# A main part played from one written list, with relu evictions over one or two PSUM banks and input loads as words of the list

## The chip, the cores and the metric

The kernel runs on one NeuronCore of one Trainium2 chip. The metric is the device time of one execution in microseconds (us). Engines are named as the profile names them: PE is TensorE (matmuls; PEld is its weight load), DVE is VectorE, ACT is ScalarE, POOL is GpSimd, SP is SyncE, which here only issues DMAs.

## The reference

Two stages follow each other. The first is induced attention on `x` (4 batches of 12544 rows of 128), with 32 inducing rows `I`:

```python
def mab(q, kv):
    s = scale * (q @ kv.transpose(0, 2, 1))
    s = s - s.max(-1, keepdims=True)
    a = np.exp(s)
    a /= a.sum(-1, keepdims=True) + 1e-09
    return a @ kv
h = mab(I, x)
return mab(x, h)
```

The second takes the 50176 resulting rows, with three weights, as

```python
h1 = x @ w1
h2 = x @ w2
g = np.maximum(h1, h2)
return g @ w_out
```

where `w1` and `w2` are 128x1024 and `w_out` is 1024x128. The output is 50176x128 in float32.

## The kernel before, in words

**Algebra.** max(h1, h2) = h1 + relu(h2 - h1), so the second stage is x·(w1·w_out) + relu(x·(w2 - w1))·w_out. As a row of the attention's output is (weights over 32 inducing rows) @ h, divided by its denominator, `w2 - w1` and `w1·w_out` are first multiplied by h (32 rows): `hwd` and `m1`. Per chunk of 128 rows PE then makes 8 relu inputs (128 x 128 each) from the exponentials `e2` (32 rows deep) and `hwd`, evicts them from PSUM with relu to f16, multiplies the 8 relu tiles with the 8 pieces of `w_out` on the full array and accumulates them in one PSUM region, adds the linear part `e2·m1`, divides by the denominator in the last eviction and stores.

**Tiling.** A batch has 98 chunks. Chunks are staged in 28 blocks of up to 16 chunks: one block's scores are made by four column tiles of PE (`stage`, 128x32 tiles) and exponentiated by ACT into one `e2` tile in which row quarter q (partitions 32q to 32q+31) holds up to four chunks. The relu inputs of the four quarters are made side by side by four row tiles (32x128) of PE. One *unit* is one PSUM bank (512 f32 columns) of relu inputs of one quarter; 784 units in all. A *group* is the chunks of one quarter of one block: up to four chunks in one output bank, 8 products per chunk; 108 groups, 3136 products. PSUM has 8 banks, `psall[:, 0..7, :]`, which units, groups, stages and all the rest share. PE changes its tile shape between products (128x128), units (32x128) and stages or scores (128x32).

**Phase 1 of the next batch** runs within the main part of the current one: seven loads of x (POOL's queue, float32 in DRAM to f16), DMA transposes of x into `xT` (SP's queue, words `x`), scores against the inducing rows (`c`), DMA transposes of their exponentials (`t`), sums (`a`), the rest (`r`), then small steps (`e`, `h`, `w`, `m`) that give `hwd` and `m1`. Batch 0 has its phase 1 in a head of its own, before 22 us.

**What sets the order.** Every engine runs its instructions in the order in which the kernel records them (`tc.manual_schedule`), and waits for others by semaphores. Before, the order of the main part comes from `ORDER`, a string of words, together with a planner: `Clock` estimates when each engine and bank is free; `phase(n, vector)` picks up to n quarters that have a unit to make, the bank that is free first for each, and an order of matmuls by estimated tile times, with a bit of `vector` per unit for its evicting engine (DVE or ACT); a number N means N products (`final_one`); `keep_busy` puts filler matmuls on `warm` in front of products that the clock expects to wait; `bank()` takes the bank that the clock holds to be free first. Weight steps (`weights_3`, and the third step of `small_hwd(0, ...)`) put fillers too. `relu_out` can evict two neighbouring banks as one instruction where a unit is held for the next (`hold`), but no word of `ORDER` asks for it: before, all relu evictions are of one bank.

**Denominators.** For most blocks a DMA transpose of `e2` (SP) feeds five additions and one power with exponent -1 on POOL (`turn_e2`, words `g`); for the others PE multiplies `e2` with a matrix of ones and DVE takes the reciprocal (`dens`). Group evictions (`evict_group`) wait for them; `EVICT` says for each group whether DVE evicts it in one instruction (0) or ACT in one per chunk (1). Six output buffers `osbs` are stored from SP's queue.

**Loads before.** All seven loads of batch b+1 for b = 1 and 2 are issued in a row at the end of the last sum (`pool_accum`, `last`), behind a copy into `pace` on POOL that waits for that sum. The loads of batch 1 are issued in the head.

Lines that the steps below touch: 840 and 619 (warm-up and filler matmuls), 662 (product of the weights), 712 (stage), 945 (filler of `keep_busy`), 989 (products), 1205 (units and linear part), 1110 and 1107 (relu eviction on ACT and DVE), 1024 and 1031 (group eviction on DVE and ACT), 776 and 780 (POOL's denominators), 228 (loads), 241 (transposes of x).

Of the kernel before, what the change touches and what calls it, by code (L numbers as in the profile page):

```python
# [9 lines left out]
F16 = mybir.dt.float16  # L10
# [6 lines left out]
INF = 1e9  # L17
# [90 lines left out]
class Quarter:  # L108


    def __init__(self, b, c0, w):
        self.b, self.c0, self.w = b, c0, w
        self.subs = {1: [1], 2: [2], 3: [2, 1], 4: [4]}[w]


class Block:


    def __init__(self, quarters, full=()):
        self.quarters = quarters  # L120
        self.width = max(qu.w for qu in quarters if qu)
        self.b = [qu.b for qu in quarters if qu][0]
        self.staged = None
        self.first = None
        self.divided = 0.0
        self.rp = None
        self.units = []
        self.done = {}
        self.relu = {}
        self.last_group = {}  # L130
        self.groups = []
        for q, qu in enumerate(quarters):
            jobs = []
            t0 = 0
            for w in qu.subs if qu else []:
                for u in range(2 * w):
                    jobs.append((q, t0, w, u))
                t0 += w
            self.units.append(jobs)
            if qu:  # L140
                self.groups.append(Group(self, [(q, t) for t in range(qu.w)], q in full))


class Group:
    def __init__(self, blk, chunks, full):
        self.blk, self.chunks, self.full = blk, chunks, full
        self.q = chunks[0][0]
        self.bank = self.ps = None
        self.started = self.linear = False
        self.order, self.parts = [], []  # L150
        for q, t0, w, u in blk.units[self.q]:
            jpb = 4 // w
            self.parts.append((t0, u))
            self.order += [(jpb * u + jj, t0 + t) for jj in range(jpb) for t in range(w)]
# [3 lines left out]
def kernel(  # L158
# [37 lines left out]
    relus = [big.tile([128, 2, 4096], F16, name=f"relus{q}", tag=f"relus{q}") for q in range(4)]  # L196
    relu1 = [big.tile([128, 1024], F16, name=f"relu1_{q}", tag=f"relu1_{q}") for q in range(2)]
    osbs = big.tile([128, NOUT, 4, C], F32, name="osbs", tag="osbs")

# [23 lines left out]
    def load_x(b, i, after=None):  # L223
        k0, n = parts[b][i]
        if after is not None:

            nc.gpsimd.tensor_copy(out=pace, in_=after)
        nc.gpsimd.dma_start(out=xn_at[b, i][:, 0:n, :], in_=xr[b, :, k0 : k0 + n, :])  # L228
        if b:
            issued = ck.on_pool(ck.pe, 0.55)  # L230
            if i == 0 and b > 1:
                ck.loading = issued - 0.55
            st[b]["ld", i] = ck.loading + 6.3 + 2.72 * i if b > 1 else 25.7 + 2.5 * i
# [4 lines left out]
    def transpose_x_dma(b, j):  # L238
# [3 lines left out]
        landed = ck.on_sp(st[b]["ld", i], "x7" if n == 7 else "x14")  # L242
        for k in range(k0, k0 + n):
            st[b]["T", k] = landed

    identity16 = consts.tile([128, 128], F16, name="identity16")
    head16 = relus[3][:, 0, :]
# [10 lines left out]
    wf = relus[0][:, 0, :].bitcast(F32)  # L258
    w1f, w2f = wf[:, 0:J], wf[:, J : 2 * J]
    w1s = relus[1][:, 0, :]  # L260
# [8 lines left out]
    pace = consts.tile([128, 1], F32, name="pace")  # L269

    with tc.manual_schedule(engines={ET.PE, ET.DVE, ET.Activation, ET.Pool, ET.SP}):

        xf = relus[2][:, 0, 0 : 256 * P1].bitcast(F32)
# [119 lines left out]
        def pool_scores(b, u):  # L393
            if u == 0:
                st[b]["es"] = smp.tile([128, NU], F32, name=f"es_{b}", tag="esu")
            bi, ps = bank([128, 512])
            ck.wait(ck.bank[bi], "p1")
# [10 lines left out]
            ck.feed(8)  # L408
            end = ck.run(0.226, "col")
            if u % 2 == 0:  # L410
                st[b]["pair", u // 2] = etp.tile([128, 2, 512], F16, name=f"eu_{b}_{u}", tag="eu", bufs=3)
            eu = st[b]["pair", u // 2][:, u % 2, :]
            nc.scalar.activation(  # L413
                out=eu, in_=ps, func=AF.Exp, scale=scale, accum_out=st[b]["es"][:, u : u + 1]
            )
            ck.bank[bi] = ck.on_act(end, 0.575)
            st[b]["eu", u] = eu, ck.bank[bi]

        def pool_rest(b):

            bi, ps = bank([128, 512])
            ck.wait(ck.bank[bi], "p1")
# [900 lines left out]
```

## Time and profile before

| | |
|---|---|
| median of 3 runs | 314.52 us (314.47 to 314.9) |
| the profiled execution's span, first to last instruction | 312.9 us |
| mean granted PE clock | 0.998 |
| PE busy | 306.0 us (98%), 5316 matmuls |
| ACT busy | 280.7 us (90%) |
| DVE busy | 273.1 us (87%) |
| POOL busy | 122.6 us (39%) |

How rows are read. A group of instructions has "xcount | busy us, mean ns of one | idle time before them and what ended it". A row of waits has the waiting engine and line, what it waited for, and us in total, times, longest. A row of the timeline has start, duration from the first to the last of merged instructions, engine, line and operation; its duration holds the pipeline's depth, so starts are compared with starts. A row of stretches has the stretch, then busy time and count for PE, PEld, DVE, ACT and POOL, then the granted PE clock, the DMA engines' share and GB/s. A busy PE is a PE with a matmul in its pipeline.

### The profile page before, as it was taken

The page shows a single profiled execution, that of the slowest core. Times are in us where ns is not written, and L with a number is a line of the kernel's source. Part 1 is how long each engine was busy: PE and PEld are TensorE (multiplying, and loading weights), DVE is VectorE, ACT ScalarE, POOL GpSimd, SP SyncE. Part 2 cuts the span into 40 slices and gives each one's busy share as a digit, 9 for nine tenths or more (in the row PEclk, how much of TensorE's full clock was granted, in tenths as well). Part 3 has the DMA queues.
Part 4 walks back from the last instruction along what each step waited for, and adds up shares of the span by engine and source line. Part 5 has one row for each costly group of instructions (what it writes and reads, how often), then busy time and mean ns, then how long its engine had stood idle before and what let it go on. Part 6 is the DMA issues. An engine that isn't in the chain of part 4 may idle for free.

```text
span 312.9 us, 12567 instructions
## 1 busy us (share of the span) xinstructions
PE 306.0 (98%) x5316; PEld 239.4 (77%) x5316; DVE 273.1 (87%) x485; ACT 280.7 (90%) x581; POOL 122.6 (39%) x183
## 2 busy tenths in 40 slices
PE   6999999999999999999999999999999999999996
PEld 2875777777877777778877887778778877788885
DVE  2458999999889999988999998999999899989894
ACT  3668999999989989999999999989999899998875
POOL 7374007910530006677500565139205743288000
PEclk9999999999999999999999999999999999999999
DMA  7999999999399999989699999993422522342223
GB/s 206 208 255 203 218 214 192 167 231 232 107 204 244 256 212 202 212 199 218 136 241 256 185 241 200 194 229 114 131 86 103 153 102 87 118 130 103 103 88 136
DMA packets 80793, 55.69 MB, mean 178 GB/s; under 512 B 62272, under 2 KB 65632, under 8 KB 80736
## 3 DMA queue, kind: packets, MB, share of 16 engines
q1 hardware_dynamic: 74768, 41.19, 56.5%
q0 software_dynamic: 5968, 13.70, 22.6%
q8 instruction: 41, 0.67, 0.9%
q14 instruction: 16, 0.13, 0.1%
HBM read 27.28 MB, written 25.69 MB: 169 GB/s over the span
## 4 chain that ended last, share of the span: by engine, by line
PE 94%; DMA 3%; DVE 1%; issue 1%; POOL 0%; ACT 0%; POOLq 0%
PE psall L989 61%; PE psall L1205 23%; DMA xn<-in_x_dram 3%; PE psall L712 2%; PE psall L458 1%; PE psall L399 1%; PE psall L309 1%; PE psall L371 1%; PE psall L325 1%; DVE relus L1107 1%; PE psall L571 1%; PE psall L504 0%; PE psall L362 0%; DVE hwd L575 0%; PE psall L819 0%
## 5 line engine op out<-in xcount | busy, mean ns | idle before, releaser
L1110 ACT ACTIVATE relus<-psall 128x512 f16<-128x512 f32 x468 | 239.2, 620 | 15.4 <-PE psall L1205 14.4
L1107 DVE TENSOR_SCALAR relus<-psall 128x512 f16<-128x512 f32 x308 | 195.5, 683 | 16.6 <-PE psall L1205 15.7
L989 PE MATMUL psall<-woutp,relus 128*128 128x128 f16 x3104 | 203.7, 220 | 0.0
L989 PEld LDWEIGHTS <-relus 128*128 128x128 f16 x3104 | 174.9, 98 | 33.1 <-issue 27.3
L1205 PE MATMUL psall<-e,hwd 32*128 32x512 f16 (+2 forms) x840 | 81.1, 362 | 0.0
L776 POOL TENSOR_TENSOR half<-ed 128x256 f32<-128x256 f16 (+2 forms) x22 | 13.4, 611 | 145.5 <-DMA ed<-e 145.5
L780 POOL TENSOR_TENSOR rd<-den,minus 128x16 f32<-128x16 f32 (+2 forms) x22 | 57.8, 2628 | 1.7
L1024 DVE TENSOR_TENSOR osbs<-psall,rd 128x512 f32<-128x512 f32 (+1 forms) x80 | 50.9, 637 | 4.3 <-PE psall L1205 1.3
L1205 PEld LDWEIGHTS <-hwd 32*128 32x128 f16 x880 | 27.9, 91 | 11.7 <-issue 2.3
L1205 PE MATMUL psall<-m,e 32*128 32x128 f16 x372 | 36.6, 216 | 0.0
L1205 PEld LDWEIGHTS <-e 32*128 32x128 f16 x372 | 22.2, 92 | 9.6 <-issue 2.0
L776 POOL TENSOR_TENSOR half<-half 128x32 f32<-128x32 f32 (+4 forms) x66 | 21.4, 324 | 5.2
L228 POOL DMA_DIRECT2D xn<-in_x_dram x32 | 17.8, 569 | 5.7 <-DMA xn<-in_x_dram 4.3
L1024 DVE TENSOR_TENSOR osbs<-psall,rp 128x512 f32<-128x512 f32 (+3 forms) x24 | 15.6, 649 | 0.5 <-PE psall L1205 0.4
L313 DVE COPY xT<-psall 128x512 f16<-128x512 f16 (+3 forms) x12 | 5.7, 485 | 8.6 <-PE psall L309 8.4
L413 ACT ACTIVATE eu<-psall 128x512 f16<-128x512 f32 x18 | 10.8, 612 | 0.3 <-PE psall L399 0.2
L725 ACT ACTIVATE e<-psall 128x512 f16<-128x512 f32 (+2 forms) x21 | 10.9, 574 | 0.1
L316 ACT COPY xT<-psall 128x768 f16<-128x768 f16 (+3 forms) x10 | 5.8, 576 | 4.6 <-PE psall L309 4.5
L309 PE MATMUL psall<-identity,xn 128*128 128x128 f16 x98 | 7.5, 219 | 1.5 <-DMA xn<-in_x_dram 1.0
L712 PE MATMUL psall<-xT,hT 128*32 128x512 f16 (+3 forms) x110 | 8.4, 362 | 0.0
L309 PEld LDWEIGHTS <-xn 128*128 128x128 f16 x98 | 5.5, 97 | 3.1 <-DMA xn<-in_x_dram 1.4
L399 PE MATMUL psall<-xT,inducingT 128*32 128x512 f16 x72 | 6.4, 381 | 0.0
(114 smaller groups left out, 129.8 us busy)
## 6 DMA issues: line engine op xcount, KB each, us to landing
out_dram<-osbs SPq DMA_DIRECT2D x90, 256.0 KB, 2.9
xn<-in_x_dram POOLq DMA_DIRECT2D x24, 448.0 KB, 9.9
out_dram<-osbs SPq DMA_DIRECT2D x10, 128.0 KB, 4.3
relus<-in_moe_w_dram POOLq DMA_DIRECT2D x4, 256.0 KB, 5.7
xn<-in_x_dram POOLq DMA_DIRECT2D x4, 224.0 KB, 10.3
xT<-xn SPq DMA_TRANSPOSE x33, 4.3
relus<-in_x_dram SPq DMA_DIRECT2D x1, 512.0 KB, 4.0
relus<-in_x_dram SPq DMA_DIRECT2D x1, 384.0 KB, 4.4
```

What stands on the lines that cost most here:

```text
L228: nc.gpsimd.dma_start(out=xn_at[b, i][:, 0:n, :], in_=xr[b, :, k0 : k0 + n, :])
L309: nc.tensor.transpose(ps[:, j, :], xn[:, g + j, :], identity16)
L413: nc.scalar.activation(out=eu, in_=ps, func=AF.Exp, scale=scale, accum_out=st[b]["es"][:, u : u + 1])
L712: nc.tensor.matmul(out=ps[32 * q : 32 * (q + 1), 128 * t : 128 * (t + n)], lhsT=hq, rhs=xT[:, c : c + n, :], start=True, stop=True, tile_p ...
L725: nc.scalar.activation(out=blk.e2[:, 0 : 128 * wd], in_=ps[:, 0 : 128 * wd], func=AF.Exp, scale=st[0]["rs"] if blk.b == 0 else scale,)
L776: nc.gpsimd.tensor_tensor(out=dst, in0=cur[:, :, 0:n], in1=cur[:, :, n : 2 * n], op=ALU.add)
L780: nc.gpsimd.tensor_tensor(out=rp[:, 0:wd, :].rearrange("p t q -> p (t q)"), in0=den[:, 0 : 4 * wd], in1=minus1[:, 0 : 4 * wd], op=ALU.pow,)
L989: nc.tensor.matmul(out=g.ps[lo:hi, 128 * c : 128 * (c + 1)], lhsT=relu[:, lo:hi], rhs=woutp[:, jb, :], start=not g.started, stop=(state["m ...
L1024: nc.vector.tensor_mul(osb[:, 0:m, :], g.ps[:, 0 : m * C].rearrange("p (s c) -> p s c", s=m), g.blk.rp[:, t0 : t0 + m, q : q + 1].broadcas ...
L1107: nc.vector.tensor_scalar(out=dst, in0=src, scalar1=0.0, scalar2=None, op0=ALU.max)
L1110: nc.scalar.activation(out=dst, in_=src, func=AF.Relu)
L1205: nc.tensor.matmul(**seq.pop(0))
```

## The change

The planner's part in the main loop goes. `ORDER` becomes `PLAN`, a list in which each word names all that was chosen before: a visit `pQBe...` names for each unit the quarter Q, the bank B and the end of its eviction (`a` ACT, `v` DVE, `+` together with the next unit, as one instruction over both banks), `l` or `L` adds the linear part of the current or of a held group, and digits after a colon give the order in which the quarters' matmuls alternate; `dN` are N products, `oB` opens a group's bank, `nB` makes denominators on PE, `sB`, `cu.B` and so on carry their bank. `l2.0` to `l3.6` are the single loads of batches 2 and 3, `x` the transposes and `g` the turns of denominators as before, at other places. The loads no longer follow the last sum, and the copy into `pace` is gone. `keep_busy` and the fillers of `weights_3` and the last `hwd` step are gone (the words `H3.0.0` and `W4.0` ask for 0 of them).

A pair may join units of different quarters and banks that do not neighbour each other: the relu tiles become one tile `slots` of 64 pieces of 512 columns, and a pair is a strided access on both sides.

```diff
-    relus = [big.tile([128, 2, 4096], F16, name=f"relus{q}", tag=f"relus{q}") for q in range(4)]
+    slots = big.tile([128, 64, 512], F16, name="relus", tag="relus")
...
-    def load_x(b, i, after=None):
+    def load_x(b, i):
         k0, n = parts[b][i]
-        if after is not None:
-
-            nc.gpsimd.tensor_copy(out=pace, in_=after)
         nc.gpsimd.dma_start(out=xn_at[b, i][:, 0:n, :], in_=xr[b, :, k0 : k0 + n, :])
...
-            if last and b + 1 < B:
-                for i in range(7):
-                    load_x(b + 1, i, acc[:, C : C + 1] if i == 0 else None)
...
+        def relu_out(parts, vector):
+            if len(parts) == 2:
+                (a, ba), (z, bz) = [(home[1] + unit[2], bi) for home, unit, bi, _, _ in parts]
+                assert a < z and ba < bz
+                dst = slots[:, a : z + 1 : z - a, :]
+                src = psall[:, ba : bz + 1 : bz - ba, :]
+            else:
+                (home, _), (t0, w, u), bi, w4, _ = parts[0]
...
+            if vector:
+                nc.vector.tensor_scalar(out=dst, in0=src, scalar1=0.0, scalar2=None, op0=ALU.max)
+            else:
+                nc.scalar.activation(out=dst, in_=src, func=AF.Relu)
...
+            busy, turns = [0] * 4, [int(c) for c in turns]
+            while any(seq for _, _, seq in rows):
+                k = min((k for k in range(len(rows)) if rows[k][2]), key=lambda k: busy[rows[k][0]])
+                k = turns.pop(0) if turns else k
+                q, cols, seq = rows[k]
+                nc.tensor.matmul(**seq.pop(0))
+                busy[q] += cols
...
-        ORDER = """
-        s p4.9 s p2.2 H1 V W p2.2 p4.2 14 m0 p3.1 4 p3.2 4 p3.3 15 p4.2 6 x1.0 2 p3.6 15 p4.8 13 p4.5 14
...
+        PLAN = """
+        s6 p05v p10+31a p17v s2 p24a H3.0.0 V6.5 p00+11a27v:22010010 p12v23v:1010 x1.0 W4.0 p06a25a37a x1.1 l2.0
+        o2 d1 m0.0 d3 n1 d4 o6 d3 p24a33vLl x1.2 p00v11a35a d13 o2 d4 p07a14v33al x1.3 p21v p30v p05+36a:10 d15
...
+        p24a36vLl s7 p01v13a22v30a d15 g17 p34a p06a17a21v d13 o3 d5 g15 p02a20vl p04v11a26a:102 d1 g16 d2 o5 d5
+        l3.6 d9 x3.8 p17v32al p00v11v24a d10 p06a12+23a37a d8 o4 d8 x3.9 d9 p00+11vl p02a15+26a33a:2013 d15 o7
...
-        EVICT = "000000000000000000000000000000000000000000000000000000000000000000000000000000000000000000000000000000101101"
+        EVICT = "000000000000000000001000001101000000000101000000000000000000001000000000000000000000000000000000000010101110"
```

Counted in the two recorded orders: of the 784 units 280 are evicted in pairs (94 pairs on ACT, 46 on DVE) and 504 singly (277 and 227; before 473 and 311). Output pieces that ACT evicts go from 10 to 37, group evictions on DVE from 104 to 96. POOL turns one block's denominators more (23 instead of 22) and PE those of four chunks fewer.

896 lines of the change are left out of this document (336 added, 560 removed).

## The prediction

> **What bounds the kernel now.** I read the page's busy shares and chain first, then what TensorE (PE) waited for, then engine busy time by stretch, then the timeline of PE.
>
> ```profile
> span 312.9 us, 12567 instructions
> ...
> PE 94%; DMA 3%; DVE 1%; issue 1%; POOL 0%; ACT 0%; POOLq 0%
> ```
> ```profile
> PE psall L840 <- DVE ones_q L292: 1.2, 1, 1.2
> PE psall L309 <- DMA xn<-in_x_dram: 1.0, 2, 0.8
> PE psall L662 <- DVE relus L646: 0.5, 1, 0.5
> ```
> ```profile
> 32.00:100.00 68.00, 68.00 (x1197) 52.21 (x1194) 63.26 (x110) 65.22 (x136) 21.51 (x32) 1.00 1.01 200
> 100.00:200.00 100.00, 100.00 (x1720) 77.86 (x1719) 92.34 (x158) 95.21 (x199) 39.91 (x56) 1.00 1.01 212
> 200.00:300.00 100.00, 100.00 (x1762) 81.26 (x1760) 92.09 (x160) 92.01 (x188) 43.71 (x60) 1.00 0.44 125
> ```
>
> The chain that sets the end is PE for 94%. The longest waits of PE by name are a few tenths to 1.2 us, the last being the first product of the weights (L662, at 26.56 below); in the main part no wait on a relu eviction reaches this list. From 32 to 300 us PE is busy throughout (second number of a row), VectorE (DVE) and ScalarE (ACT) some 92 to 96%, GpSimd (POOL) under half. So an eviction that gets cheaper shortens nothing by itself. What counts is the length of PE's own stream, the start before 28 us, and waits that a new order may bring.
>
> A busy PE may still have gaps, so the timeline is read start to start:
>
> ```profile
> 273.18 0.39 PE L1205 MATMUL psall<-e,hwd 32*128 32x512 f16 x4
> 273.50 1.35 PE L989 MATMUL psall<-woutp,relus 128*128 128x128 f16 x21
> 274.78 0.23 PE L1205 MATMUL psall<-m,e 32*128 32x128 f16 x1
> ...
> 275.32 1.90 PE L989 MATMUL psall<-woutp,relus 128*128 128x128 f16 x31
> 277.16 0.23 PE L1205 MATMUL psall<-m,e 32*128 32x128 f16 x1
> ...
> 277.70 1.74 PE L989 MATMUL psall<-woutp,relus 128*128 128x128 f16 x28
> 279.37 0.39 PE L1205 MATMUL psall<-e,hwd 32*128 32x512 f16 x4
> ```
>
> L989 are the products with w_out on the full array, L1205 the stretches of relu inputs on four row quarters. 31 products and the change of mode after them take 277.16-275.32 = 1.84 us, 21 take 1.28: 0.056 us each, 0.10 for the change. A row stretch of one unit per quarter (512 columns) takes 273.50-273.18 = 0.32, one of two units 277.70-277.16 = 0.54: about 0.10 for the change and 0.055 per 128 columns of its fullest quarter; a quarter that stays empty saves nothing. These numbers fill the stretch without a gap: there is hardly a stall to remove.
>
> **The change part by part.** All 3136 products and 784 relu units stay; PE has ten matmuls fewer, four for denominators and six fillers.
>
> *PE's stream.* I counted stretches of equal tile shape in the two instruction orders, from the weights' product to the end. Full stretches 160 before, 147 after: -13 x 0.10 = -1.3 us. Row stretches 162 and 149: -13 x 0.10 = -1.3. Their fullest quarters add up to 958 and 976 times 128 columns: +18 x 0.055 = +1.0, as the list packs some stretches less evenly. Stretches of column tiles 22 and 27: +5 x 0.10 = +0.5, taken at the cost of a row stretch. Four denominator matmuls and a filler fewer: -0.2, from these rows:
>
> ```profile
> 27.65 0.25 PE L819 MATMUL psall<-ones_q,e_first 128*128 128x4 f16 x4
> ...
> 27.98 0.22 PE L945 MATMUL psall<-warm 128*128 128x128 f16 x1
> ```
>
> Sum -1.3 us, and as PE is never covered by another engine here, all of it would be on the path. Bounds: -2.2 if a column stretch costs nothing more and every filled gap counts, -0.6 if the looser stretches cost one more change each.
>
> *The start.* The fillers that the planner put in go, and row work stands there instead.
>
> ```profile
> 23.18 0.69 ACT L725 ACTIVATE e<-psall,rs 128x512 f16<-128x512 f32 x1
> 24.16 0.61 PE L619 MATMUL psall<-warm 128*128 128x512 f16 x2
> 25.26 0.81 PE L619 MATMUL psall<-warm 128*128 128x512 f16 x3
> 25.77 0.62 ACT L649 COPY relus<-psall 128x512 f16<-128x512 f16 x1
> 26.09 0.41 DVE L646 COPY relus<-psall 128x512 f16<-128x512 f16 x1
> 26.56 0.62 PE L662 MATMUL psall<-woutp,relus 128*128 128x128 f16 x8 [0.48 <-DVE relus L646]
> 27.57 4.03 ACT L1110 ACTIVATE relus<-psall 128x512 f16<-128x512 f32 x8
> ```
>
> Removing five fillers looks like 1 us (0.81-0.61 = 0.20 each), but PE waited for the copies of the turned weights anyway: DVE's ended last, at 26.50. ACT's new order there is e, a two-bank relu, e, a single relu, then the weights' copy. Eight singles in 4.03 us with a last one of 0.62 start every 0.49, so 0.13 of each duration lies under the next. With starts 0.56 (e), 0.92 (two-bank, below), 0.56, 0.49 and the copy's 0.62, the copy ends at 23.18+3.15 = 26.33; DVE has one relu fewer ahead of its copy and is done earlier. I take 26.33-26.50 = -0.2 us; bounds -0.8 (three more stretches of relu units already stand finished when the products begin) and +0.6 (ACT a pair later, with m's matmul queued behind it on PE).
>
> *Two-bank evictions.* 94 pairs on ACT, 46 on DVE, 504 singles. No row shows a 128x1024 f32 eviction. Nearest rows:
>
> ```profile
> L1110 ACT ACTIVATE relus<-psall 128x512 f16<-128x512 f32 x468 | 239.2, 620 | 15.4 <-PE psall L1205 14.4
> L1107 DVE TENSOR_SCALAR relus<-psall 128x512 f16<-128x512 f32 x308 | 195.5, 683 | 16.6 <-PE psall L1205 15.7
> ...
> L316 ACT COPY xT<-psall 128x768 f16<-128x768 f16 x4 | 3.2, 799 | 2.6 <-PE psall L309 2.6
> ...
> L1031 ACT ACTIVATE osbs<-psall,rd 128x128 f32<-128x128 f32 x10 | 3.1, 383 | 2.0 <-issue 1.0 <-PE psall L963 0.9
> ...
> L313 DVE COPY xT<-psall 128x1024 f16<-128x1024 f16 x4 | 2.8, 692 | 4.7 <-PE psall L309 4.7
> ```
>
> ACT: the 768-column copy is 0.18 us over a 512-column single, 0.70 ns a column: 0.98; with 0.83 from the smaller copies 1.05. Upper bound two singles, 1.24. I take 1.05. DVE: lower bound the half-width copy, 0.69, upper 1.37; the slope between its 128- and 512-column evictions is near 1.04 ns, so 1.22. A pair starts the next 0.92 later where two singles take 0.98: 94 x 0.06 = 5.6 us of ACT time saved, of which 27 more output pieces (0.38 each with 0.13 hidden, 6.8 us) take all. Neither is on the path. What is, is delay: the earlier bank of a pair comes free 0.43 us later on ACT (1.05-0.62), 0.54 on DVE. For every eviction that PE waits on I took the PE work between the matmul read and the PE instruction that needs the result, less the eviction's duration. Of 826 singles before, the median slack is 0.97 us and 57 have under 0.3. After, 133 pairs have a median of 0.62 and 20 under 0.3, 558 singles 0.92 and 41; four are negative by 0.26 us together. So stalls of 0.3 us at least; with queues on two engines at 92% I take +0.5. Bounds: -0.3 (the small gaps of before go) and +3.5 (the 20 tight pairs lose 0.15 each on top).
>
> The Trainium skill, "VectorE: DVE Perf Modes", section on the TRN2 errata, prices a PSUM read on ScalarE at 172 cycles fixed plus one per column at 1.2 GHz; by that estimate a pair lasts 1.00 us and saves 0.14, 13.4 us of ACT in all. The 0.49 starts say that most of the fixed part is hidden already, so the page's saving would leave the sum as it is and only shorten queues.
>
> *Loads.* The seven loads of batches 2 and 3, issued in a row before, now stand singly in POOL's queue, so a load can wait behind denominators, and SP's transposes and stores behind the load.
>
> ```profile
> 48.09 0.66 POOL L776 TENSOR_TENSOR half<-ed 128x256 f32<-128x256 f16 x1 [21.29 <-DMA ed<-e]
> ...
> 50.38 2.94 POOL L780 TENSOR_TENSOR rd<-den,minus 128x16 f32<-128x16 f32 x1
> 53.30 0.66 POOL L776 TENSOR_TENSOR half<-ed 128x256 f32<-128x256 f16 x1
> ```
> ```profile
> DMA to landing us min/median/max: 4.9/12.3/19.1
> ...
> DMA to landing us min/median/max: 2.9/4.3/9.1
> ```
>
> The two landing rows are those of the 14 loads of batches 2 and 3, and of the transposes into xT. A turn of denominators takes 53.30-48.09 = 5.2 us. The tightest place: batch 3's last load stands behind four turns placed near 161 to 170 us, so it issues near 165+4x5.2 = 186. In the bursts of before the loads took 4.9 us (the first) to 19.1 (the last); alone I take 4.9, so it lands at 191. Its transpose, placed at 183, holds SP until then with the stores behind it, and lands 4.3 later, at 195; PE needs it near 201. Six output buffers with an eviction each 2.6 us (108 groups in 280 us) cover those 8 us of held stores. Cost 0, with 6 us to spare; 2 us if the load takes the bursts' median; if the cover goes, PE waits at the last columns' scores. All other transposes are placed 5 to 69 us ahead of their use, more than before. The removed pace copies were on POOL, off the path.
>
> *Tail.* The last eviction moves from ACT (0.38) to DVE: -0.1.
>
> **Sum:** -1.3-0.2+0.5-0.1 = -1.1 us, 311.8 for the profiled execution's 312.9. The runs' median is 1.6 above that span, so 314.52-1.1 = 313.4 us.
>
> **The rivals.** *Pairs hold banks too long (slower).* PE's next unit finds its bank still held. For it: both engines at 92% and the shorter slack of pairs; against: ACT and DVE do slightly less in all. Without stalls the sum is -1.6, so it decides from 1.6 us of them on; at the bound of +3.5 the sum is +1.9, 316.4; middle 315.7.
>
> *Gain given back (no change).* Stalls of 1.0 to 2.2 us eat the shorter stream: 314.5. For it: before runs without gaps because fillers and planned waits surround them; against: similar numbers of tight waits.
>
> *A late load.* If the last load takes the bursts' longest 19.1 us, its transpose lands near 209, 8 us late: 321.4. Against: it stands alone.
>
> *Clock.* Without fillers PE idles about 1 us at the start. The row shows 1.18 us of work in 2 us at a clock of 1.00:
>
> ```profile
> 6.00:8.00 2.00, 1.18 (x13) 0.52 (x11) 0.69 (x1) 1.27 (x2) 1.12 (x3) 1.00 1.04 206
> ```
>
> At half rate for the 3.4 us until the fourth group the time would be near 316. The Trainium skill, "TensorE: Matmul & The Clock Gate", section "What's actually happening", has the clock halve after an idle window of about 3.4 us; the row's shorter gap agrees with no change.
>
> **How the numbers follow.** Forecast (312.4 to 313.9) 0.51; no change 0.23; held banks 0.20; late load 0.03; clock 0.03. About 0.2%, 0.6 us, is what a measurement can tell from no change: faster is under 313.9, slower over 315.15. That gives faster 0.51, same 0.23, slower 0.26. The range leaves out the upper half of held banks and the two rare cases, and the best tail: 312.3 to 316.0.
>
> **What would show it.** Right: PE's waits still without a relu eviction of note after 28 us, 0.32 and 0.54 us stretches unchanged, the weights' product near 26.4, two-bank evictions near 1.05 and 1.22 us. Wrong: row stretches or full products with tenths of a microsecond of idle before them, released by ACT or DVE; PE idle near 201 us behind a transpose; a granted clock under 1.00 before 40 us.

## The result, and the profile after

| | kernel before | kernel after |
|---|---|---|
| time, median (range, runs) | 314.61 us (314.47 to 314.9, 4) | 337.0 us (334.08 to 341.32, 4) |
| ratio, 95% interval | | 1.062 (1.060 to 1.064) |
| span of the profiled execution | 312.9 us | 339.5 us (its time 341.32) |

The change costs some 20 us. The four runs of the changed kernel spread over 7 us, so every ratio in this document is made from a kernel's quicker runs; the profiled execution here is the longest of the four.

Line numbers are now those of the changed kernel: L426 are the sums (words `a`), which read the transposed exponentials `eT`, L411 the DMA transposes into `eT` (words `t`), L224 those of x, L945 units and linear part, L889 and L891 the relu evictions on VectorE and ScalarE, L860 the output evictions on VectorE, L874 the stores and L216 the loads. In later runs they are shifted by the lines that an edit adds, and in runs of the kernel before they follow that kernel.

The page of the changed kernel, its span, three lines of its slices (40 equal parts, tenths), its chain, and the group of the sums that read `eT`:

```profile
span 339.5 us, 12514 instructions
...
PE   7999979999179999993999999979999999999996
...
PEclk9999998999769999997899999998999999999999
DMA  8999999999997999999689939494332336332233
...
PE 72%; DMA 16%; DVE 4%; ACT 2%; POOL 2%; issue 2%; SPq 0%; POOLq 0%; ACTq 0%; DVEq 0%
...
L426 PE MATMUL psall<-xn,eT 128*32 128x128 f16 x288 | 6.3, 240 | 16.8 <-DMA eT<-eu 16.8
```

PE is idle in holes (the 7, 1, 3 and 7 of its line) with its clock lowered in or behind each. DMA now has 16% of the chain, where it had 3%. The view of waits names them (total, count, longest in us):

```profile
PE psall L426 <- DMA eT<-eu: 16.8, 4, 9.4
PE psall L945 <- DVE relus L889: 1.8, 2, 1.6
```

Four waits, before the sums `a`, are for `eT` transposes. Only 1.8 us stand under relu evictions, and their origin is a DMA too (below). The same stretches as before, busy times by engine (PE, PEld, DVE, ACT, POOL), clock, DMA share, GB/s:

```profile
32.00:100.00 68.00, 56.54 (x941) 43.51 (x938) 49.74 (x81) 49.96 (x92) 11.87 (x16) 0.90 1.12 195
100.00:200.00 100.00, 94.03 (x1583) 72.61 (x1578) 84.28 (x130) 87.23 (x163) 39.60 (x58) 0.97 0.97 180
200.00:300.00 100.00, 98.00 (x1675) 77.12 (x1675) 88.41 (x137) 89.05 (x151) 49.38 (x65) 0.98 0.50 133
```

ACT and DVE have room now; they wait for PE. The chain of waits in order of time at the longest hole (start, length, what), and behind it the landing times of all `eT` transposes, from the view of that tile, after and before:

```profile
81.48 0.23 ACT eu L393
81.71 0.03 ACT relus L891
81.74 14.12 DMA eT<-eu
...
95.90 1.04 PE psall L426 x32
```
```profile
DMA to landing us min/median/max: 3.1/4.7/14.1
```
```profile
DMA to landing us min/median/max: 3.2/4.1/5.4
```

The third `eT` transpose of batch 1 was issued at 81.74, at once after its input was written, and landed 14.1 us later; in the kernel before the slowest took 5.4. So the transpose wasn't asked for late; it ran slowly. What ran beside it, by the DMA view from 82 to 96 us:

```profile
DMA packets 2123, 2.19 MB, mean 156 GB/s; under 512 B 1401, under 2 KB 1401, under 8 KB 2121
...
xn<-in_x_dram POOLq DMA_DIRECT2D x2, 448.0 KB, 15.8
out_dram<-osbs SPq DMA_DIRECT2D x2, 256.0 KB, 15.5
xT<-xn SPq DMA_TRANSPOSE x2, 15.5
eT<-eu SPq DMA_TRANSPOSE x1, 14.1
```

Two loads (l3.0, l2.4) were issued at 82.26 and 83.04. The first of them had waited 13.1 us in POOL's queue for the second sums of batch 1, which still read its buffer, and so came out together with the next `eT`.

The other holes have the same root at other places. Near 47 us PE waited 1.6 us for a relu eviction, which stood behind an output eviction, which waited 2.5 us for a store (first fence, VectorE's timeline: start, length, idle before). That store stood in SP's queue behind two x transposes held from 26.12 on (second fence, SP's timeline), which were in flight beside batch 1's loads and two of batch 2:

```profile
47.55 0.69 DVE L860 TENSOR_TENSOR osbs<-psall,rp 128x512 f32<-128x512 f32 x1 [2.50 <-DMA out_dram<-osbs]
```
```profile
26.12 13.76 SPq L224 DMA_TRANSPOSE xT<-xn  x2
39.93 2.28 SPq L874 DMA_DIRECT2D out_dram<-osbs  x1
```

At 153.4 PE waited 5.4 us for the first `eT` of batch 2, issued beside l3.2 and l3.3. At 226 it waited 1.8 us for the first `eT` of batch 3; this one is the late load of the prediction. The timelines of POOL (the load, issued when four turns of denominators had ended), SP (the x transpose that waited for it, with four stores and the `eT` transpose behind it) and PE:

```profile
213.93 0.61 POOL L216 DMA_DIRECT2D xn<-in_x_dram  x1
```
```profile
218.74 1.54 SPq L224 DMA_TRANSPOSE xT<-xn  x1
220.68 2.20 SPq L874 DMA_DIRECT2D out_dram<-osbs  x4
222.98 2.25 SPq L411 DMA_TRANSPOSE eT<-eu  x1
```
```profile
227.74 0.63 PE L426 MATMUL psall<-xn,eT 128*32 128x128 f16 x32 [1.77 <-DMA eT<-eu]
```

Last, the clock. Windows of the changed kernel around the first two holes; the column after POOL is PE's granted clock:

```profile
47.30:50.90 3.60, 1.83 (x26) 1.28 (x25) 3.35 (x6) 1.60 (x3) 0.00 (x0) 1.00 0.98 260
50.90:54.30 3.40, 3.40 (x36) 2.68 (x34) 2.89 (x5) 1.94 (x2) 0.00 (x0) 0.50 1.09 209
...
88.40:95.90 7.50, 0.00 (x1) 0.01 (x2) 0.00 (x0) 0.34 (x1) 0.00 (x0) 0.50 1.36 130
95.90:98.60 2.70, 2.70 (x52) 2.61 (x53) 0.42 (x2) 0.00 (x0) 0.00 (x0) 0.50 1.45 93
```

PE works on at half clock for 3.4 us behind the first hole, 2.7 behind the second, 4.6 and 3.4 behind the others. The account of the profiled execution: 9.4+5.4+1.8+0.2 us of waits for `eT`, 1.8 for the relu evictions, 0.6 for a bank near 145 us, together 19.2; and at most half of 14.1 us at half clock, 7.0. That is 26.2 of the 339.5-312.9 = 26.6 us.

### The profile page after: what moved, and what is told of

Read it like the earlier page. It is cut to its first block, busy times and chain, and to the rows that moved or that the text cites. A ratio compares the mean times of both kernels' runs of the same rounds, so it can differ in the third digit from the quotient of the medians.

```text
span 339.5 us, 12514 instructions
## 1 busy us (share of the span) xinstructions
PE 313.9 (92%) x5306; PEld 244.4 (72%) x5306; DVE 270.9 (80%) x439; ACT 280.0 (82%) x506; POOL 127.2 (37%) x187
## 4 chain that ended last, share of the span: by engine, by line
PE 72%; DMA 16%; DVE 4%; ACT 2%; POOL 2%; issue 2%; SPq 0%; POOLq 0%; ACTq 0%; DVEq 0%
PE psall L827 46%; PE psall L945 18%; DMA eT<-eu 9%; DMA ed<-e 3%; DMA out_dram<-osbs 2%; DMA xn<-in_x_dram 2%; DVE relus L889 2%; PE psall L637 1%; PE psall L426 1%; DVE osbs L860 1%; PE psall L381 1%; PE psall L288 1%; ACT relus L891 1%; POOL half L690 1%; POOL rd L694 1%
## 5 line engine op out<-in xcount | busy, mean ns | idle before, releaser
L891 ACT ACTIVATE relus<-psall 128x512 f16<-128x512 f32 (+1 forms) x367 | 232.4, 715 | 37.7 <-PE psall L945 36.0
L889 DVE TENSOR_SCALAR relus<-psall 128x512 f16<-128x512 f32 (+1 forms) x269 | 197.0, 776 | 26.7 <-PE psall L945 26.1
L827 PEld LDWEIGHTS <-relus 128*128 128x128 f16 x3104 | 178.0, 99 | 32.0 <-issue 28.3
L945 PE MATMUL psall<-e,hwd 32*128 32x512 f16 (+2 forms) x840 | 83.0, 366 | 1.9 <-DVE relus L889 1.8
L690 POOL TENSOR_TENSOR half<-ed 128x256 f32<-128x256 f16 (+2 forms) x23 | 14.1, 612 | 158.8 <-DMA ed<-e 158.8
L694 POOL TENSOR_TENSOR rd<-den,minus 128x16 f32<-128x16 f32 (+2 forms) x23 | 60.8, 2643 | 1.8
L860 DVE TENSOR_TENSOR osbs<-psall,rd 128x512 f32<-128x512 f32 (+2 forms) x78 | 50.3, 645 | 6.3 <-ACT osbs L867 2.4
L945 PEld LDWEIGHTS <-hwd 32*128 32x128 f16 x880 | 28.9, 91 | 16.7 <-issue 5.7
L945 PE MATMUL psall<-m,e 32*128 32x128 f16 x372 | 36.6, 219 | 0.0
L945 PEld LDWEIGHTS <-e 32*128 32x128 f16 x372 | 22.0, 94 | 7.3 <-issue 1.5
L216 POOL DMA_DIRECT2D xn<-in_x_dram x32 | 18.2, 576 | 18.4 <-PE psall L426 13.1
L690 POOL TENSOR_TENSOR half<-half 128x64 f32<-128x64 f32 (+4 forms) x69 | 22.4, 325 | 5.4
L426 PE MATMUL psall<-xn,eT 128*32 128x128 f16 x288 | 6.3, 240 | 16.8 <-DMA eT<-eu 16.8
L426 PEld LDWEIGHTS <-eT 128*32 128x32 f16 x288 | 4.9, 106 | 18.7 <-DMA eT<-eu 18.1
L393 ACT ACTIVATE eu<-psall 128x512 f16<-128x512 f32 x18 | 10.8, 611 | 7.2 <-PE psall L381 7.0
L860 DVE TENSOR_TENSOR osbs<-psall,rp 128x512 f32<-128x512 f32 (+3 forms) x18 | 11.5, 640 | 3.0 <-DMA out_dram<-osbs 2.5
L458 DVE TENSOR_TENSOR hacc<-psall,hacc 128x128 f32<-128x128 f32 (+1 forms) x6 | 1.7, 289 | 10.3 <-PE psall L445 9.8
L867 ACT ACTIVATE osbs<-psall,rd 128x128 f32<-128x128 f32 x29 | 8.5, 382 | 0.9 <-issue 0.9
## 6 DMA issues: line engine op xcount, KB each, us to landing
xn<-in_x_dram POOLq DMA_DIRECT2D x4, 224.0 KB, 10.3
```

Source lines behind the costliest of these rows:

```text
L393: nc.scalar.activation(out=eu, in_=ps, func=AF.Exp, scale=scale, accum_out=st[b]["es"][:, u : u + 1])
L426: nc.tensor.matmul(out=ps[32 * g : 32 * (g + 1), 0:128], lhsT=eT[:, 4 * (v % 2) + j, 32 * g : 32 * (g + 1)], rhs=xn_of(b, U * v + 4 * g + ...
L690: nc.gpsimd.tensor_tensor(out=dst, in0=cur[:, :, 0:n], in1=cur[:, :, n : 2 * n], op=ALU.add)
L694: nc.gpsimd.tensor_tensor(out=rp[:, 0:wd, :].rearrange("p t q -> p (t q)"), in0=den[:, 0 : 4 * wd], in1=minus1[:, 0 : 4 * wd], op=ALU.pow,)
L827: nc.tensor.matmul(out=g.ps[:, 128 * t : 128 * (t + 1)], lhsT=home[:, 128 * (jb * w4 + t) : 128 * (jb * w4 + t + 1)], rhs=woutp[:, jb, :], ...
L860: nc.vector.tensor_mul(osb[:, 0:n, :], g.ps[:, 0 : n * C].rearrange("p (s c) -> p s c", s=n), blk.rp[:, 0:n, q : q + 1].broadcast_to((128, ...
```

## The experiments

Three theories were held against each other. *Shared DMA engines*: loads in flight starve the DMA transposes beside them, so these and all that stands behind them in SP's queue come late. *Two-bank evictions*: pairs hold their banks too long. *List*: the written order itself is longer, or its transposes stand too few words ahead of their use. Ratios are to the kernel before, measured on the same chip in the same session.

**The changed kernel again** (no edit).

> The changed kernel once more, for a second trace beside the experiments. Theory 'shared DMA engines' (loads that are in flight starve the DMA transposes that run beside them, so eT comes late, TensorE idles and its clock is halved): 334 to 341 us, TensorE waits for DMA eT<-eu 10 to 20 us in 3 to 5 places, half clock behind each long wait. Theory 'two-bank evictions' (banks are held too long): the same time, but the waits on relu evictions should then show more than 5 us in all. Theory 'list' (t words stand too few words ahead of their sums): the same time and the same waits as the first.

335.49 us median (333.15 to 341.32), ratio 1.0636 (1.0591 to 1.0681). This trace has 10.6 us of waits for `eT` instead of 16.8, but 4.6 instead of 0.6 us for a bank whose output eviction comes late and 3.3 instead of 1.8 us under relu evictions, and again 339.5 us of span. The sum is steady, the place isn't.

**Pairs split.**

```diff
-                relu_out(made[k : k + n], made[k + n - 1][4] == "v")
+                for p in made[k : k + n]:
+                    relu_out([p], made[k + n - 1][4] == "v")
```

> The changed kernel with every two-bank relu eviction split into two single ones on the same engine; loads, list and queues stay. 'Shared DMA engines' and 'list': 333 to 342 us, with the waits for eT at the same places. 'Two-bank evictions': below 320 us.

338.56 us (333.5 to 343.07), ratio 1.0615 (1.0592 to 1.0638), the same as with pairs. PE waits for `eT` 7.5 us, for banks behind output evictions 5.1, and 2.9 us near 132 for which the view names no releaser. The waits aren't all at the same places as with pairs (below), but the time is, so pairs aren't the cause.

**Loads in rows again.** The l words of a batch stand together behind the last sums of the batch before, with the small copy that held them back; the x words of batches 2 and 3 stand behind them.

```diff
-        ... l3.0 a1.5.4 x2.1 l2.4 ...
+        ... a1.5.4 l2.0 l2.1 l2.2 l2.3 l2.4 l2.5 l2.6 ...
```

> The list of the changed kernel with one part undone: the seven loads of batch 2 and of batch 3 go out in a row again, each row behind the last sums of the batch before, and the x transposes of these batches stand behind them; everything on TensorE, VectorE and ScalarE is as in the changed kernel. 'Shared DMA engines': eT lands 3 to 6 us after its issue everywhere, TensorE's waits for eT fall below 1 us, the clock stays 1.00, 312 to 315 us. 'Two-bank evictions': above 330 us. 'List': the eT waits stay above 10 us in all, above 328 us.

339.05 us (337.15 to 339.76), ratio 1.0764 (1.073 to 1.080): the time went the wrong way, the mechanism as expected. The waits for `eT` are gone (first fence: landing of `eT`), but PE waits as much elsewhere (second fence: waits):

```profile
DMA to landing us min/median/max: 3.0/4.0/5.7
```
```profile
PE psall L948 <- DVE osbs L863: 10.9, 2, 5.7
PE psall L401 <- DMA xT<-xn: 8.6, 1, 8.6
```

The list puts the ed transposes of denominators where the rows of loads now run. That of block 6, issued at 84.93, landed at 95.94; POOL's turn ended at 99.5, and VectorE, in order, held its relu evictions behind an output eviction that needed it (the 8.6 us, behind x transposes of batch 3 whose words this list had moved back, weren't followed further):

```profile
99.52 0.42 DVE L863 TENSOR_TENSOR osbs<-psall,rd 128x256 f32<-128x256 f32 x1 [5.94 <-POOL rd L697]
```

So the victim changes with the place of the loads; an order is right or wrong for loads, x, ed and eT words together.

**The mechanism in the kernel before.** Four of its loads go out some 8 us earlier, in the g6 step ahead of POOL's own part, and are left out of the row behind the sums:

```diff
+            if blk is blocks[6]:
+                nc.gpsimd.tensor_copy(out=pace, in_=st[1]["eT", 3][0][:, 7, 127:128])
+                for b, i in early:
+                    k0, n = parts[b][i]
+                    nc.gpsimd.dma_start(out=xn_at[b, i][:, 0:n, :], in_=xr[b, :, k0 : k0 + n, :])
```

> The kernel before with one thing added to its order: the first four loads of batch 2 go out when the second eT transpose of batch 1 has landed (about 77 us) instead of behind the last sums (about 85 us), so that they are in flight when the third eT transpose is issued (about 79 us). No two-bank eviction, no list. 'Shared DMA engines': that eT lands at 87 to 92 us instead of 82.1, TensorE idles 4 to 8 us before its sums, 319 to 326 us. 'Two-bank evictions' and 'list': no change, 314 to 315 us.

324.68 us (324.39 to 325.02), ratio 1.0316 (1.0299 to 1.0333): as expected by the first theory alone. The `eT` landed at 91.35, 12.7 us after its issue, and PE waited 8.2 us (timeline of PE):

```profile
91.40 1.05 PE L461 MATMUL psall<-xn,eT 128*32 128x128 f16 x32 [8.19 <-DMA eT<-eu]
```

The queues in the DMA view: packets, MB, share of 16 engines; q0 is POOL's queue of loads, q1 SP's of transposes and stores. First this run from 82 to 88 us, then the kernel before from 79 to 82, where no load runs:

```profile
q0 software_dynamic: 364, 1.16, 98.3%
q1 hardware_dynamic: 269, 0.07, 8.1%
```
```profile
q1 hardware_dynamic: 1182, 0.49, 67.6%
```

Without loads SP's queue gets 1182/3 = 394 packets through in a microsecond, beside loads 269/6 = 45, where the loads get 364/6 = 61. A load's packet carries 1.16 MB/364, 3.2 KB; a transpose's 0.07 MB/269, 0.26 KB. So in these 6 us SP's queue moves 0.07 MB and the loads 1.16. The Trainium skill, "DMA: Bandwidth & Descriptors", section on queues, rings and completion order, states that each engine goes round its queues packet by packet. The counts of this trace from 84 to 88 us, 238 packets of SP's queue beside 241 of the loads, agree with turns of one for one; those from 80 to 82 us, 21 beside 108, don't, and the trace doesn't show why.

**Smaller packets.** The four early loads are cut into halves of seven columns.

```diff
-                    nc.gpsimd.dma_start(out=xn_at[b, i][:, 0:n, :], in_=xr[b, :, k0 : k0 + n, :])
+                    for lo in (0, 7):
+                        nc.gpsimd.dma_start(out=xn_at[b, i][:, lo : lo + 7, :], in_=xr[b, :, k0 + lo : k0 + lo + 7, :])
```

> The kernel before with the four early loads, each cut into two of seven columns, so that a packet of a load has 1,792 bytes instead of 3,584. If the DMA engines take one packet of a load and one of a transpose in turn, the third eT transpose gets twice as many turns: it lands at 86 to 89 us instead of 91.35, TensorE idles 3 to 6 us instead of 8.2, 319 to 323 us. If a transpose just waits for the bytes that were asked for before it, nothing changes: eT at 91 us, 324 to 326 us.

324.21 us (322.9 to 326.48), ratio 1.0308 (1.0254 to 1.0363): by time not told from the run before. In the trace the `eT` landed at 89.46, short of the 86 to 89 expected, and PE waited 6.1 us instead of 8.2. Queues from 84 to 88 us:

```profile
q0 software_dynamic: 355, 0.56, 84.7%
q1 hardware_dynamic: 351, 0.09, 23.6%
```

351/4 = 88 packets a microsecond for SP against 355/4 = 89 of loads: one for one, and half as many again as the 238/4 = 60 of the run before in the same stretch. In other stretches it isn't one for one: 657 beside 325 from 80 to 84 us here, 1858 beside 263 from 82 to 96 in the changed kernel. So turns of one packet each are seen in one stretch of two traces; how the engines share otherwise, and that smaller packets pay, is not shown.

**What the half clock costs.** 34 idle matmuls ahead of the waiting sums of that kernel.

```diff
+            if b == 1 and last:
+                for _ in range(34):
+                    nc.tensor.matmul(out=ps, lhsT=warm[:, 0:128], rhs=warm, start=True, stop=True)
```

> The kernel before with the four early loads, and 34 idle matmuls (7.5 us) on TensorE ahead of the sums that wait for the third eT transpose, so that TensorE does not stand still there. eT lands as late as in the run without the fillers. If the half clock behind the wait costs time of its own, no window of half clock is left and the time falls by 1.5 to 2.5 us, to 322 to 323.2 us. If it costs nothing, the time stays at 324.4 to 325.0 us.

324.07 us (323.4 to 329.16), ratio 1.0284 (1.0261 to 1.0307) against 1.0316 (1.0299 to 1.0333). No window of half clock is left. From the first of the waiting sums to PE's last matmul it took 318.12-91.45 = 226.7 us instead of 319.72-91.40 = 228.3 (start times in the two traces): 1.6 us for 3.7 us at half clock. With the wait of 8.2 us that makes 9.8 of the 323.0-312.9 = 10.1 us that the four early loads cost. The time fell by only some 1.0 us, less than expected, and the intervals touch.

**One place at a time.** Two loads behind the next ed word; then the last load ahead of the denominators; then the two earliest loads later:

```diff
-        ... l3.0 a1.5.4 x2.1 l2.4 d12 o2 d1 e1.7 p14v25a36al d2 g6 ...
+        ... a1.5.4 x2.1 d12 o2 d1 e1.7 p14v25a36al d2 g6 l2.4 l3.0 ...
```

> The changed kernel with two words moved: the loads 0 of batch 3 and 4 of batch 2 stand behind the next ed word in GpSimd's queue instead of around the last sums of batch 1. 'Shared DMA engines': the longest wait (9.4 us, for the third eT of batch 1) goes, the waits for the eT of batches 2 and 3 stay, 321 to 330 us. 'List': 333 to 341 us.

337.43 us (330.94 to 341.75), ratio 1.0579 (1.0495 to 1.0664). The hole of 9.4 us shrank to 1.0, but 4.8 us for a bank behind an output eviction came near 135, and 6.5 instead of 5.4 before the first sums of batch 2. By time nothing is shown. Nor do the moved words alone explain the short hole: in the runs with split pairs, with the last load ahead and with the two earliest loads later, both loads keep their words, and yet the same `eT` landed after 6.1, 6.2 and 5.8 us. What differs is when the first of the two loads went out. In those runs it was 1.8, 1.6 and 1.6 us after the transpose was issued (fence: the run with the last load ahead, timelines of SP and POOL); in the changed kernel's two traces, where the `eT` landed after 14.1 and 10.6 us, it was 0.5 and 0.3 us. (Here, with both loads gone from there, the `eT` took 4.7.)

```profile
81.84 1.71 SPq L411 DMA_TRANSPOSE eT<-eu  x1
```
```profile
83.43 0.54 POOL L216 DMA_DIRECT2D xn<-in_x_dram  x1 [14.27 <-PE psall L426]
```

So in these five traces a microsecond in the start of one load goes with a transpose that takes 6 us or 10 to 14, and the runs of one kernel can differ by such a hole.

```diff
-        ... g14 ... g17 ... g15 ... g16 d2 o5 d5 l3.6 ...
+        ... l3.6 g14 ... g17 ... g15 ... g16 d2 o5 d5 ...
```

> The changed kernel with one word moved: the last load of batch 3 stands ahead of the four turns of denominators in GpSimd's queue instead of behind them. 'Shared DMA engines' together with the order of the queues: the wait of 1.8 us for the first eT of batch 3, which was issued late behind the transpose that waited for this load, goes with its 3.4 us of half clock; 2 to 4 us less than the changed kernel, the other three waits stay. 'List' without the queues: no change.

333.1 us (332.2 to 334.92), ratio 1.0585 (1.055 to 1.0621). The wait before the first sums of batch 3 went with its half clock. The five traces in which this load stands behind the turns of denominators (the changed kernel twice, pairs split, and the two runs beside this one) all have that wait, of 1.2 to 2.4 us: this is the late load, undone by one word. The time doesn't show it, as the intervals of the ratios overlap, and the waits ahead of the moved word, which were expected to stay, changed too: 3.0 us for `eT` in all, 6.6 for banks behind output evictions.

```diff
-        ... x1.1 l2.0 ... l2.1 ... d15 l2.2 ...
+        ... x1.1 ... d15 l2.0 l2.1 l2.2 ...
```

> The changed kernel with two words moved: the loads 0 and 1 of batch 2, which go out near 27 us, stand beside the loads 2 and 3, near 68 us. 'Shared DMA engines': the wait of 1.6 us near 47 us (a store held behind an x transpose that was starved by these loads) goes; in its place four loads are in flight when the first two eT transposes of batch 1 are issued, which land 8 to 14 us after their issue instead of 4.7 and 6.2; the time stays within 333 to 341 us. 'List': no change in the waits.

332.98 us (329.08 to 337.2), ratio 1.0533 (1.0464 to 1.0603): the median is at the lower end of what was expected. The wait near 47 us went. Of the two `eT` transposes the first landed after 8.4 us, as expected; the second was issued only at 79.4 behind the queue and landed after 5.0, which wasn't; and a wait of 4.3 us for an x transpose of batch 1 came at 78.

**Loads kept apart from what is needed soon**, first in rows of three and four placed by hand, then tied to landings. The second kernel has a word of its own:

```diff
+        def pool_gate(b, u):
+            nc.gpsimd.tensor_copy(out=pace, in_=st[b]["eT", u][:, 7, 127:128])
...
+        ... t1.5 k1.5 l2.0 l2.1 l2.2 l2.3 l2.4 l2.5 l2.6 ...
+        ... t2.1 k2.1 l3.0 l3.1 g11 ...
+        ... g13 t2.3 t2.5 k2.5 l3.2 l3.3 l3.4 l3.5 l3.6 g12 ...
```

> The changed kernel with its loads in rows of three or four, so placed that no load should be in flight when an eT transpose or an ed transpose that is soon needed is issued; the x transposes of batches 2 and 3 and six ed words move with them; TensorE, VectorE and ScalarE do what they do in the changed kernel. 'Shared DMA engines': TensorE's waits fall below 3 us in all, the clock stays near 1.00 in the main part, 312 to 317 us. 'List' (the written list is itself longer, whatever the loads do): above 325 us.

338.73 us (336.63 to 342.23), ratio 1.0734 (1.0691 to 1.0778), a miss. The waits for `eT` fell to 0.4 us, but three loads came out at 107 and starved the x transposes of batch 2; behind them in SP's queue the ed word of block 9 came late, and PE waited 9.1 us. The x transposes of batch 3 cost 6.1 in the same way. The backlog of the queue, not just one transfer, has to be counted.

> The changed kernel with its loads tied to the eT transposes: a small copy in GpSimd's queue reads the third eT of batch 1 before the seven loads of batch 2, the first eT of batch 2 before two loads of batch 3, the third eT of batch 2 before the other five; x transposes and the ed words of blocks 6 and 8 to 17 are placed between these rows of loads in the order in which they are needed. 'Shared DMA engines': no load runs beside an eT transpose or a pressing ed transpose; waits of TensorE below 2 us in all, 312 to 316 us. 'List': above 325 us.

319.03 us (317.5 to 323.09), ratio 1.0115 (1.0083 to 1.0148): above the expected 312 to 316 us, but below the 325 that the list theory asked for. Some 16 us of the loss are gone (ratio 1.062 to 1.0115) with the same instructions on PE, VectorE and ScalarE. 5.3 us of waits for `eT` are left, where less than 2 was expected, with two windows of half clock.

**What is left, and the worth of pairs.** The first `eT` of batch 2 moves ahead of that batch's last x transpose, one load less stands behind it, and the x words of batch 3 start earlier; then the same with pairs split.

```diff
-        ... x2.10 ... t2.1 k2.1 l3.0 l3.1 g11 ... g13 t2.3 t2.5 k2.5 l3.2 ...
+        ... t2.1 k2.1 l3.0 x2.10 g11 ... t2.3 t2.5 g13 k2.5 l3.1 l3.2 ...
```

> The kernel with gated loads once more, with three things moved: the first eT transpose of batch 2 goes ahead of the last x transpose of that batch, one load instead of two stands between it and the next eT, and the x transposes of batch 3 start earlier. 'Shared DMA engines': the waits for eT that were left (0.6, 1.8 and 2.7 us, two of them with 3.4 us of half clock) fall below 1.5 us in all, 313.5 to 317 us. If what is left lies in the list itself, the time stays at 317.5 to 320 us.

> The same kernel with every two-bank relu eviction split into two single ones on the same engine. If two-bank evictions are worth as little as the prediction put them (bounds -0.3 to +3.5 us for pairs): within -3.5 to +0.5 us of the run with pairs. If pairs save time that the starved transposes hid: 1 to 5 us slower than with pairs.

With pairs 323.25 us (317.31 to 325.76), ratio 1.0079 (1.0057 to 1.0101); split 324.56 us (321.39 to 329.45), ratio 1.0262 (1.0223 to 1.0302). The times still move with late transposes: the profiled execution with pairs, 317.31 us, kept its clock at 1.00 and waited 2.6 us for `eT`, more than the 1.5 expected; four of its six runs took 322 us or more at clocks of 0.984 to 0.989, so the ratio with pairs rests on two runs. So the list is compared where nothing waits, over the same products: all up to 6/16 of them, and the last 6/16. Products alone, in windows that begin and end with the same product; the first number behind the window is its length. Kernel before, with pairs, split:

```profile
26.60:136.20 109.60, 77.28 (x1159) 65.17 (x1160) 1.00 1.03 206
209.20:309.60 100.40, 75.85 (x1187) 66.63 (x1184) 1.00 0.36 112
```
```profile
26.20:136.30 110.10, 76.02 (x1160) 65.29 (x1160) 1.00 1.00 205
212.00:312.10 100.10, 74.83 (x1184) 66.45 (x1182) 1.00 0.36 109
```
```profile
26.20:137.00 110.80, 76.05 (x1159) 65.31 (x1160) 1.00 1.00 202
220.60:321.70 101.10, 74.80 (x1183) 66.43 (x1183) 1.00 0.35 107
```

Together 210.0, 210.2 and 211.9 us. The last gated kernel below, with pairs, has 110.1 and 100.2, together 210.3. The list without waits is as long as the order before, and pairs save 1.7 us over three quarters of the products: within the 1 to 5 us slower that was expected for split pairs, though from a single trace with pairs split.

**The sums later, and two ed words moved.** a2.3, a2.5 and a3.1 go one stretch back; then g13 behind the loads and g17 behind t3.1.

```diff
-        ... a3.1.6 c3.2.2 c3.3.5 t3.3 o7 d15 ... a2.3.2 a2.5.4 p10a23v36vl d1 p25a ...
+        ... c3.2.2 c3.3.5 t3.3 o7 d15 a3.1.6 ... p10a23v36vl d1 p25a a2.3.2 a2.5.4 ...
```

> The kernel with gated loads and its three moves, and in it the sums that still waited (the second and third of batch 2, the first of batch 3) stand one stretch later in TensorE's order. 'Shared DMA engines': the 2.6 us that TensorE still waited fall below 1.2 us in the profiled run; its undisturbed runs reach 314.5 to 316.5 us, the level of the kernel before, and not less, as the list without waits takes as long as the order before. If the predicted 1.1 us are in the list after all: 313 to 314.2 us.

321.0 us (317.6 to 321.79), ratio 1.0155 (1.0114 to 1.0195), a miss: the sums of batch 2 don't wait any more, but the x transposes of batch 3 were later in this execution, and the `eT` behind them made PE wait 3.4 us.

> The last version with two ed words moved: that of block 13 stands behind the six loads of batch 3 in GpSimd's queue (so these go out 2 to 3 us sooner), that of block 17 behind the first eT transpose of batch 3. 'Shared DMA engines': the wait of 3.4 us for that eT and its window of half clock go, TensorE waits less than 1.2 us in the main part, the profiled execution takes 312.5 to 315 us of span and the runs 314 to 317 us: no shorter than the kernel before. If the predicted 1.1 us are in the list: a span below 312.2 us, runs of 313 to 314 us.

318.19 us (316.79 to 320.58), ratio 1.0089 (1.0064 to 1.0114). 2.0 us of waiting at that same place are left, with 3.4 us of half clock, where less than 1.2 and none were expected; span and median are above what was expected too. No version here beats the kernel before.

## Why the prediction was wrong

The likeliest case was 313.4 us in a range of 312.3 to 316.0; it came to 337.0.

*The step that failed* is in the part on loads: "Cost 0, with 6 us to spare". It asked whether a load is in time for its transpose, and answered from landing times of a kernel that mostly kept them apart: the row of loads from 85 to 107 us there had no transpose beside it until the x transposes began at 106. "Alone I take 4.9" for a load, and 4.3 for a transpose, don't hold beside each other: 15.8 us for a load, 14.1 for an `eT`, 20.3 for an x transpose. "All other transposes are placed 5 to 69 us ahead of their use" was of little help: the third `eT` of batch 1 had 4.8 us, from 81.74 to 86.50, enough for the median of 4.1 us of before and not for 14.1. The load was priced as a thing that might be late; what it does to others wasn't priced. The run that puts four loads beside one `eT` of the kernel before shows this with neither pairs nor list: +10 us. The runs with gated loads give some 16 us back.

The warning stood in the prediction's own row, "2.9/4.3/9.1": the 9.1 us belong to an x transpose that the kernel before issued at 32.92, while loads of batch 1 were in flight, and the next one landed after 7.5. Its DMA view from 30 to 36 us (packets, MB, share; last, us to landing):

```profile
q0 software_dynamic: 376, 1.21, 101.4%
q1 hardware_dynamic: 112, 0.06, 4.6%
...
xT<-xn SPq DMA_TRANSPOSE x1, 9.1
```

The prediction took the median, 4.3, and left the longest aside.

*A late load* was named as a rival at 3%, with the right place (behind four turns of denominators) and the right turn, 5.2 us. The load went out at 213.93, 4 x 5.2 behind 193.2. It cost 1.8 us and a window of half clock, not 8 us. The rival was too narrow: one load that waits, instead of all loads that run beside transposes.

*Clock.* The rival put it at the start, where the clock did stay at 1.00; it appeared behind the holes instead, for at most 7 of the 26.6 us.

*Held banks.* No. Pairs last as estimated, 1.05 and 1.22 us forecast for 1,030 and 1,220 ns measured (groups of the changed kernel by shape):

```profile
L891 ACT ACTIVATE relus<-psall 128x1024 f16<-128x1024 f32 x94 | 95.2, 1030 | 9.6 <-PE psall L945 9.5
L889 DVE TENSOR_SCALAR relus<-psall 128x1024 f16<-128x1024 f32 x46 | 56.0, 1220 | 8.4 <-PE psall L945 8.1
```

What PE lost in its row stretches (next paragraph) lies within the bounds for their stalls, -0.3 to +3.5; against single evictions in the same list pairs save time.

*PE's stream*, -1.3 us forecast, and +0.5 for pairs: measured +0.2 over three quarters of the products. By the starts of the stretches in those windows, full stretches went from 118 in 143.0 us to 109 in 141.8 and column stretches from 16 in 10.3 to 19 in 10.8, both near the forecast. Row stretches went from 120 in 52.8 to 110 in 53.7: by "0.10 for the change and 0.055" they should have become some 0.3 shorter, so they took about 1.2 us more than forecast (2.7 with pairs split, at 55.2). Short waits for banks would do that, but no view of waits names them, so it isn't shown. The term with its +0.5 for stalls was mis-sized.

*The start*, -0.2 forecast: the weights' product came 26.23-26.56 = -0.3 us earlier.

```profile
26.23 0.62 PE L600 MATMUL psall<-woutp,relus 128*128 128x128 f16 x8
```

*Still open*: why transfers slow each other by so much, as the packet counts give no single rule; how much of the spread between runs of one gated kernel (317 to 326 us) comes from chance in the order of transfers; and what pairs would do in the kernel before, whose planner can't place them.

## What to carry to other kernels

When a change moves a DMA, ask what is in flight beside it, and price both: landing times read where transfers were kept apart don't hold where they meet. Loads and transposes shouldn't overlap if something waits for the transpose; tie the load to the landing of the transpose, and count the backlog of the whole issuing queue behind it. Read the longest landing time of a row beside its median, and ask what ran beside that one. Where PE is the bound, a hole from a late transfer can also cost clock behind it.

## What the hardware did that was not expected

In the kernel before, SP's queue fell from 394 to 45 packets a microsecond while four loads ran. In the changed kernel's longest hole it kept 1858/14 = 133, and still an `eT` took 14.1 us and the two loads beside it 15.8; nothing here shows why. Stores behind a starved transpose land late as well (15.5 us in the DMA view after).

The clock fell after holes far shorter than the 3.4 us for which it was then lowered: 1.6 us of waiting near 47.3, with PE busy for 1.83 of 3.60 us, were enough for 3.4 us of half clock from 50.9 on. The Trainium skill, "TensorE: Matmul & The Clock Gate", section "What's actually happening", asks for an idle window of about 3.4 us; the lengths of the half clock (3.4, 10.2, 6.8 and 3.4 us) agree with its window, the idle time needed doesn't. In the profiled run of the second gated list with pairs, waits of 1.0 and 1.4 us left the clock at 1.00, and so did one of 1.9 us, up to 80.03, in the run with the last load ahead: the length of a wait alone doesn't decide.
